# Sums of two gate quarters made in DRAM, and layer 2's first weights prepared at milestones, in a fused attention and two-layer kernel

## The chip, the cores and the metric

The kernel runs on one core of a Trainium2 chip. Its time is the device time of one execution in microseconds (us). Beside it stands one profiled execution, whose trace gives the start and the duration of the instructions of each engine: PE (TensorE, the matrix products), DVE (VectorE), ACT (ScalarE), POOL (GpSimd), and SP, which here only issues transfers. Each engine works through its own instructions in program order.

## The reference, cut to what matters

```python
attn = softmax(q @ k.T / 8 + cum[:, None] - cum[None, :], causal) @ v    # 4 x 8 heads, 576 positions, 64 wide
x  = attn.transpose(0, 2, 1, 3).reshape(2304, 512)
g  = leaky_relu(x @ w_in, 0.01)          # 512 -> 2048
x1 = g @ w_out                           # 2048 -> 512
h2 = x1 @ w2_in                          # 512 -> 2048
out = (h2 * sigmoid(h2)) @ w2_out        # 2048 -> 512
```

All of it is float32. The second product is `g @ w_out`; layer 2's first weights are `w2_in`.

## The kernel before, in words

A product in float32 is made of three passes in a split form: an operand is copied to a rounded high part (a cast on ACT) and the remainder is taken on DVE (`less`, line 373); high x high, high x low and low x high are added up in PSUM. The products after the first use Strassen's scheme in Winograd's form: seven products of quarters instead of eight, with sums and differences of quarters made on DVE.

The order of the instructions is written by a planner in the program itself: generators ask for an engine and a cost, wait for named signals, and a small event loop decides who issues next on each engine. So a wait that is added or dropped in one generator can move instructions of others, and the order is fixed when the program is built. Transfers issued by one engine also stand in that engine's order: one that must wait holds up the ones behind it.

The stages on PE, with lines: attention (L743, L824, L892) mixed with the first product (`hpw`, L960), to about 390 us; the second product `g @ w_out` (`acc`, L1218), from 392 us to 607 us, at first mixed with the last of the first product and at its end with the third; the third product (`m`, L1525), to 782 us; the fourth (`m`, L1667), to the end.

**The second product.** `g` is stored to DRAM (`g1_d`) by L1055 as 8 slabs (`NST`) for each of the 8 pieces of rows in `CHUNKS` (64 stores). It is read back in quarters, for three groups of 768 rows (`n` = 0, 1, 2). The quarters are named by rows and columns, 11, 12, 21 and 22; each comes in four pieces `s` (128 x 768 elements, 384 KB; the loads are L1091, tile `gq`). There is room for three quarters of a group. Quarter 21 of group n stands where 22 of group n-1 stood, and 22 where 12 stood. A piece's room is free again when its last reader is done: for 22 that is the preparation of product 4, for 12 that of product 3.

The seven products of a group are called by numbers `q` and come in the order 1, 5, 6, 2, 7, 4, 3 (1, 6, 5, 2, 7, 4, 3 from the second group on); product 1 of a group comes before products 4 and 3 of the group before it. For each, `prep` makes four split pieces in the tile `gs` (cast L1151, subtraction L373, four buffers `SPLITS`). `made` prepares two of the operands, in place: x5 = a21 + a22 (on DVE, L1117 by way of the helper line L1357) and x6 = x5 - a11 (L1120). Product 5 uses x5, product 6 uses x6, and products 2, 7 and 3 use operands built on x6. PE takes 12 matmuls of 384 columns for a piece, 6 for each half `j` of the columns. `("m1", n, j, q)` is the signal that product q of group n is made for half j.

**The weights of layer 2.** `fetch2` loads w2_in as packed words in eight pairs (two loads of 512 KB for a pair `j`, tile `wst`, L1881); `combos` decodes them (ACT L1712, DVE L1713, L1714, L1716), makes four sums and differences on DVE, and stores the pair to DRAM (`w_d<-f`, L1938, 896 KB) from one of two buffers. `fills` brings them back (`w<-w_d`, L1914) when a place is free; it also brings the 28 pieces of the second product's own weights.

**POOL** does 56 subtractions `m<-qk,m` (L369) for the heads of attention, and, after the first microseconds, nothing else.

Of the kernel before, what the change touches and what calls it, by code (L numbers as in the profile page):

```python
# [13 lines left out]
ALU = mybir.AluOpType  # L14
# [43 lines left out]
)  # L58
SPLITS = 4
INPUT_AT = 5  # L60
X_ON = "d"
SET_B = ("h", "h", ("acc", 0), ("acc", 1))


# [8 lines left out]
TB = 384  # L73
# [14 lines left out]
class Plan:  # L88
# [90 lines left out]
    def wait(self, *names):  # L179
        def step(resume):  # L180
            missing = [n for n in names if n not in self.seen]
            if not missing:
                resume()
                return
            left = [len(missing)]

            def one():
                left[0] -= 1
                if not left[0]:
                    resume()  # L190

            for n in missing:
                self.waiting.setdefault(n, []).append(one)

        return step
# [8 lines left out]
    def signal(self, name):  # L204
        self.seen[name] = True
        for fn in self.waiting.pop(name, []):
            fn()
# [79 lines left out]
def fused_kernel(ctx, tc, qt, kt, va, vb, ft, w1, wi2, wo2, out):  # L287
    nc = tc.nc
# [8 lines left out]
    SF = FF // 4  # L297
# [3 lines left out]
    NG = NT // (2 * TB)  # L301
# [389 lines left out]
    def loads():  # L691
        def line(todo):
            while todo:
                yield from load_head(todo.pop(0))

        todo = list(range(H, NSB * H))
        yield wait("cf")
        yield par(line(todo), line(todo))
# [368 lines left out]
    def quarter(grp, s):  # L1067
        return w2t["q", Q_AT[grp] + s // 2][:, s % 2]

    def q_group(n, name):  # L1070
        return {"11": 0, "21": 1 + n % 2, "12": 1 + n % 2, "22": 2 - n % 2}[name]

    def quarters():

        yield wait("decoded")
        todo = [(0, "11"), (0, "21"), (0, "22")]
        for n in range(NG):
            todo += [(n, "12")]
            if n + 1 < NG:
                todo += [(n + 1, "11"), (n + 1, "21"), (n + 1, "22")]  # L1080
        for n, name in todo:
            i, j = int(name[0]) - 1, int(name[1]) - 1
            o = (2 * n + i) * TB
            grp = q_group(n, name)
            for s in range(SF):
                sg = j * SF + s
                yield wait(*[("g1", k, sg) for k, (o1, n1) in enumerate(CHUNKS) if o1 < o + TB and o1 + n1 > o])
                yield take(("q", grp, s), 1)

                def load(n, name, s, sg, o, t):  # L1090
                    yield dma(393e3, lambda: nc.sync.dma_start(out=t, in_=g1_d[sg, :, :, o:o + TB]), 0)  # L1091
                    signal(("q", n, name, s))

                p.start(load(n, name, s, sg, o, quarter(grp, s)))

    g_order = sorted((7 * n + pos, n, q) for n in range(NG) for q, pos in G_TURN[n])
    gx = {}
# [14 lines left out]

    def made(n, s):

        a11, a21, a22 = (quarter(q_group(n, k), s) for k in ("11", "21", "22"))
        yield wait(("q", n, "21", s), ("q", n, "22", s))
        yield sub(2 * TB, a21, a21, a22, X_ON, 0, ALU.add)  # L1117
        signal(("x5", n, s))
        yield wait(("gx", n, 1, s))
        yield sub(2 * TB, a11, a21, a11, "d", 0)  # L1120
        signal(("x6", n, s))
        q_used(n, "21", s, 2)

    def prep(n, q, s, i):
        a = {k: quarter(q_group(n, k), s) for k in ("11", "12", "21", "22")}
        t = w2t["s", i % SPLITS]
        src, name = None, None
        if q == 1:
            yield wait(("q", n, "11", s))
            src = a["11"]  # L1130
        elif q == 5:
            yield wait(("x5", n, s))
            src = a["21"]
        elif q == 6:
            yield wait(("x6", n, s))
            src = a["11"]
        elif q == 7:
            yield wait(("x6", n, s))
            yield wait(("x3", n, s))
            yield sub(2 * TB, a["11"], a["22"], a["11"], "d", 0)  # L1140
            src = a["11"]
        elif q == 4:
            yield wait(("q", n, "22", s))
            src = a["22"]
        elif q == 2:
            yield wait(("q", n, "12", s))
            src = a["12"]
        else:
            yield wait(("x3", n, s))
            src = a["12"]  # L1150
        yield act(2 * TB, lambda: nc.scalar.copy(t[:, 0], src), 0, 0.09)  # L1151
        yield less(2 * TB, t[:, 1], src, f32(t[:, 0]), "d", 0, PE_LAT)
        gx[n, q, s] = t, i
        signal(("gx", n, q, s))
        if q == 5:
            q_used(n, "21", s, 2)
        elif q == 7:
            q_used(n, "22", s, 2)
            q_used(n, "11", s, 1)
        elif q == 4:  # L1160
            q_used(n, "22", s, 2)
        elif q == 2:
            yield wait(("x6", n, s))
            yield sub(2 * TB, a["12"], a["12"], a["11"], "d", 0)
            yield wait(("gx", n, 6, s))
            signal(("x3", n, s))
        elif q == 3:
            q_used(n, "12", s, 1)
# [185 lines left out]
    def sub(n, dst, a, b, engines="pd", rank=1, op_=ALU.subtract):  # L1354
        return p.either([c for c in (
            ("pool", pool_cost(n), lambda: nc.gpsimd.tensor_tensor(dst, a, b, op=op_), FAVOR),
            ("dve", dve_cost(n), lambda: nc.vector.tensor_tensor(dst, a, b, op=op_), 0.0),  # L1357
        ) if c[0][0] in engines], rank)
# [515 lines left out]
    def fetch2():  # L1874
        for which in range(2):
            if which:
                yield wait(("xc", 0, 3))
            for j in range(NP):
                for e in range(2):
                    st, i_st = yield from own([128, DM, 2], I32, "wst")  # L1880
                    yield dma(524e3, lambda: nc.sync.dma_start(  # L1881
                        out=st.rearrange("p n w -> p (n w)"), in_=(wi2, wo2)[which][j + NP * e].bitcast(I32)))
                    words2[which, j, e] = st, i_st
                    signal(("words2", which, j, e))
# [73 lines left out]
    def opening():  # L1958
        first_row["i"] = yield take("stg", STG_BUFS)
        first_row["tile"] = stg(first_row["i"], [H, 2, HALF[0][1]], F32, "cfr")  # L1960
        for i in range(5):
            yield take(("w", i), 1)
        p.start(gates(cp), after_gates)
        yield from load_first()
        yield wait(*[("weighed", n) for n in range(H)])
        for i in range(5):
            give(("w", i), 0)
# [3 lines left out]
        decp["wo"] = wo_es.enter_context(tc.tile_pool(name="wop", bufs=1))  # L1971

    with tc.manual_schedule():
        for gen in (opening(), first_weights(), loads(), attention(), hidden(), quarters(), preps(), summed(), all_fills(),
                    second_input(), second_weights(), hidden2(), second_values(), summed2()):
            p.start(gen)
        p.run()
# [51 lines left out]
```

## Time and profile before

| | |
|---|---|
| time, median of 3 runs | 960.33 us (959.15 to 962.2) |
| the profiled execution's own time | 963.02 us |
| its span, first to last instruction | 961.3 us |
| granted clock of TensorE, mean | 0.994 of full speed |
| busy: PE, DVE, ACT, POOL | 98%, 78%, 64%, 6% of the span |

The profiled execution took 2.7 us longer than the median, and 1.7 us of its time lie outside its span. Busy shares of PE count matmuls that overlap and whose ends are modelled, so the number of matmuls that start in a stretch says more than the share.

### The profile page before, as it was taken

How to read it: one execution, taken by the hardware profiler on the slowest of the kernel's cores; microseconds unless marked ns; L12 is line 12 of the kernel's file. 1: busy time of each engine (PE TensorE's matmuls, PEld its weight loads, DVE VectorE, ACT ScalarE, POOL GpSimd, SP SyncE). 2: the span in 40 equal slices, each digit the busy share in tenths (PEclk: the TensorE clock that was granted, in tenths of full speed). 3: DMA queues.
4: the chain of work that ended last, by engine and by line, in shares of the span. 5: the costliest groups of instructions: out<-in, count | busy, mean ns of one | idle time of the engine just before them, and what ended most of it. 6: DMA issues, size and time to landing. Idle time of an engine off the chain costs nothing.

```text
span 961.3 us, 18261 instructions
## 1 busy us (share of the span) xinstructions
PE 940.9 (98%) x6483; PEld 891.6 (93%) x6483; DVE 753.1 (78%) x1782; ACT 610.8 (64%) x1382; POOL 56.5 (6%) x71
## 2 busy tenths in 40 slices
PE   9999999999999999999989999999999999999998
PEld 7777998999888889999989899999999999999998
DVE  6998786689688962979999779858544498888885
ACT  7978787788588854666546359547556674444442
POOL 2001221122022100000000000000000000000000
PEclk9999999999999999999999999999999999999999
DMA  7943553466777656994956685797766683544542
GB/s 202 290 136 89 165 168 95 131 227 215 243 223 241 194 166 224 370 359 161 344 206 185 221 256 177 266 325 236 287 218 208 221 261 112 152 132 139 147 127 72
DMA packets 160023, 196.80 MB, mean 205 GB/s; under 512 B 9638, under 2 KB 145982, under 8 KB 159900
## 3 DMA queue, kind: packets, MB, share of 16 engines
q1 hardware_dynamic: 159500, 195.24, 63.5%
q8 instruction: 51, 0.84, 0.3%
q10 hardware_dynamic: 432, 0.39, 0.1%
q14 instruction: 40, 0.33, 0.1%
HBM read 125.94 MB, written 69.65 MB: 203 GB/s over the span
## 4 chain that ended last, share of the span: by engine, by line
PE 68%; DVE 13%; DMA 9%; ACT 5%; issue 3%; SPq 2%; POOL 0%; DVEq 0%; ACTq 0%; POOLq 0%
PE m L1667 18%; PE m L1525 18%; PE acc L1218 10%; PE hpw L960 10%; PE sps L743 4%; PE av L892 4%; PE tps L824 3%; DMA gq<-g_d 3%; DVE gq L1357 2%; DMA wst<-in_wi_dram 2%; ACT sc L766 1%; DVE sc L723 1%; DVE gs L373 1%; ACT sc L776 1%; PE hps L960 1%
## 5 line engine op out<-in xcount | busy, mean ns | idle before, releaser
L960 PE MATMUL hpw<-ring,w 128*128 128x320 f32 (+1 forms) x1344 | 218.0, 303 | 0.1
L960 PEld LDWEIGHTS hpw<-ring,w 128*128 128x128 f32 x1344 | 191.0, 190 | 2.4 <-issue 1.4
L1218 PE MATMUL acc<-gs,w 128*128 128x384 f32 x1008 | 186.2, 344 | 7.1 <-DVE gs L373 5.4
L1218 PEld LDWEIGHTS acc<-gs,w 128*128 128x128 f32 x1008 | 180.5, 191 | 10.2 <-DVE gs L373 6.5
L1525 PE MATMUL m<-xc,w 128*128 128x384 f32 x1008 | 180.3, 339 | 0.6 <-ACT m L1551 0.6
L1525 PEld LDWEIGHTS m<-xc,w 128*128 128x128 f32 x1008 | 177.6, 188 | 1.4 <-ACT m L1551 1.0
L1667 PE MATMUL m<-w,gc 128*128 128x256 f32 x1512 | 178.6, 280 | 0.0
L1667 PEld LDWEIGHTS m<-w,gc 128*128 128x128 f32 x1512 | 178.4, 188 | 0.0
L358 ACT CAST gc<-g 128x512 fp32r<-128x512 f32 (+1 forms) x180 | 80.0, 490 | 86.7 <-DVE g L1357 52.2
L1151 ACT CAST gs<-gq 128x768 fp32r<-128x768 f32 x84 | 69.8, 836 | 61.0 <-PE acc L1218 31.2
L766 ACT ACTIVATE sc<-sc,st 128x576 f32<-128x576 f32 (+4 forms) x160 | 92.9, 581 | 24.6 <-DVE st L723 23.6
L723 DVE CUSTOM_DVE_ANT_0 sc<-sps,zmask 128x288 f32<-128x288 f32 (+4 forms) x160 | 71.0, 448 | 31.1 <-PE sps L743 23.8
L373 DVE TENSOR_TENSOR gs<-gq,gs 128x768 fp32r<-128x768 f32 x84 | 79.4, 952 | 17.5 <-ACT gs L1151 16.9
L373 DVE TENSOR_TENSOR gc<-g,gc 128x512 fp32r<-128x512 f32 (+1 forms) x180 | 89.8, 525 | 3.3 <-ACT gc L358 1.9
L824 PE MATMUL tps<-ident,sc 66*107 66x66 f32 (+3 forms) x480 | 68.0, 269 | 3.8 <-ACT sc L776 1.8
L1357 DVE TENSOR_TENSOR g<-g 128x256 f32<-128x256 f32 x144 | 58.3, 418 | 16.7 <-DMA g<-g_d 16.2
L743 PE MATMUL sps<-m,s 66*128 66x288 f32 (+9 forms) x288 | 67.4, 315 | 3.2 <-DMA g_d<-gw 1.7
L369 POOL TENSOR_TENSOR m<-qk,m 64x288 fp32r<-64x288 f32 (+1 forms) x56 | 51.4, 930 | 275.2 <-ACT m L358 145.0
L373 DVE TENSOR_TENSOR w<-w 128x512 fp32r<-128x512 f32 x84 | 55.6, 686 | 14.6 <-ACT w L1915 14.4
L824 PEld LDWEIGHTS tps<-ident,sc 66*107 66x107 f32 (+3 forms) x480 | 55.2, 151 | 10.9 <-ACT sc L776 3.6
L1915 ACT CAST w<-w 128x512 fp32r<-128x512 f32 x84 | 50.7, 620 | 19.0 <-DMA w<-w_d 18.3
L1053 ACT ACTIVATE gw<-hpw 128x320 f32<-128x320 f32 (+1 forms) x112 | 44.7, 409 | 27.0 <-PE hpw L960 23.5
(124 smaller groups left out, 1113.3 us busy)
## 6 DMA issues: line engine op xcount, KB each, us to landing
w<-w_d SPq DMA_DIRECT2D x84, 256.0 KB
gq<-g_d SPq DMA_DIRECT2D x48, 384.0 KB
g_d<-z SPq DMA_DIRECT2D x24, 768.0 KB
g<-g_d SPq DMA_DIRECT2D x36, 512.0 KB
w_d<-f SPq DMA_DIRECT2D x16, 896.0 KB
g_d<-gw SPq DMA_DIRECT2D x32, 320.0 KB
wst<-in_w_dram SPq DMA_DIRECT2D x17, 512.0 KB
g_d<-gw SPq DMA_DIRECT2D x32, 256.0 KB
```

The costliest lines, as they stand in the source:

```text
L358: ("act", act_cost(n, base), lambda: nc.scalar.copy(dst, src), 0.0),
L373: ("dve", dve_cost(n), lambda: nc.vector.tensor_tensor(dst, a, b, op=ALU.subtract), 0.0),
L723: yield dve(w, lambda: nc.vector.tensor_tensor_reduce(out=sc[0:qn, k0:k0 + w], in0=ps[0:qn], in1=zmask[0:qn, z0:z0 + w], scale=-0.125, sca ...
L743: nc.tensor.matmul(ps[0:qn], ht[x][:, qs], ht[y][:, k0:k0 + w], start=r == 0, stop=r == len(ops) - 1)
L766: yield act(kn, lambda: nc.scalar.activation(sc[0:qn, 0:kn], sc[0:qn, 0:kn], ACTF.Exp, scale=-1.0, bias=st[0:qn, 2 * i + a:2 * i + a + 1], ...
L824: nc.tensor.transpose(ps[0:k1 - k0, o:o + qn], ht["p"][i][0:qn, k0:k1], ident[0:qn, 0:qn])
L960: nc.tensor.matmul(dst, w[:, wi, c * 128:(c + 1) * 128], x(xi, c), start=(first_ and c == 0 and r == 0), stop=(c == KC - 1 and r == 2), sk ...
L1151: yield act(2 * TB, lambda: nc.scalar.copy(t[:, 0], src), 0, 0.09)
L1218: nc.tensor.matmul(dst, w[:, e, wi, j * 128:(j + 1) * 128], x[:, xi, e], start=start and s == 0 and e == 0 and r == 0, stop=stop and s == ...
L1357: ("dve", dve_cost(n), lambda: nc.vector.tensor_tensor(dst, a, b, op=op_), 0.0),
L1525: nc.tensor.matmul(dst, w[:, wi, c * 128:(c + 1) * 128], x[:, xi, c], start=start and c == 0 and r == 0, stop=stop and c == 1 and r == 2, ...
L1667: nc.tensor.matmul(banks[b][:, e], t[:, gi, a * 128:(a + 1) * 128], w[:, wi], start=begin and a == 0 and r == 0, stop=jp == NP // 2 - 1 an ...
```

## The change

Two edits, and nothing of the arithmetic but the place where one sum is made.

First, x5 = a21 + a22 is no longer made by DVE. A new generator `added` issues twelve transfers on POOL's queue (three groups by four pieces), each of which adds the 384 KB of a piece of quarter 22 to the piece of quarter 21 within DRAM (`accum_op=ALU.add`), as soon as the stores of both are done. Quarter 21 is then loaded as the sum, after a wait for that transfer; quarter 22 is still loaded, for products 4 and 7. `made` makes only x6, and no longer waits for 22.

Second, `fetch2` waits before it loads pairs 2 to 7 of w2_in, for a milestone of the second product from the table `PACE`.

```diff
-X_ON = "d"
+PACE = {2: (0, 5), 3: (0, 2), 4: (0, 7), 5: (0, 3), 6: (1, 5), 7: (1, 7)}
...
+    def g1_made(n, i, sg):
+        o = (2 * n + i) * TB
+        return [("g1", k, sg) for k, (o1, n1) in enumerate(CHUNKS) if o1 < o + TB and o1 + n1 > o]
+
+    def added():
+        for n in range(NG):
+            o = (2 * n + 1) * TB
+            for s in range(SF):
+                yield wait(*g1_made(n, 1, s), *g1_made(n, 1, SF + s))
+                yield op("pool", 1.1, lambda: nc.gpsimd.dma_start(
+                    out=g1_d[s, :, :, o:o + TB], in_=g1_d[SF + s, :, :, o:o + TB], accum_op=ALU.add), 0, 10.0)
+                signal(("sum21", n, s))
+
     def quarters():
...
-                yield wait(*[("g1", k, sg) for k, (o1, n1) in enumerate(CHUNKS) if o1 < o + TB and o1 + n1 > o])
+                yield wait(*([("sum21", n, s)] if name == "21" else g1_made(n, i, sg)))
...
-        a11, a21, a22 = (quarter(q_group(n, k), s) for k in ("11", "21", "22"))
-        yield wait(("q", n, "21", s), ("q", n, "22", s))
-        yield sub(2 * TB, a21, a21, a22, X_ON, 0, ALU.add)
-        signal(("x5", n, s))
-        yield wait(("gx", n, 1, s))
+        a11, a21 = (quarter(q_group(n, k), s) for k in ("11", "21"))
+        yield wait(("q", n, "21", s), ("gx", n, 1, s))
         yield sub(2 * TB, a11, a21, a11, "d", 0)
...
         elif q == 5:
-            yield wait(("x5", n, s))
+            yield wait(("q", n, "21", s))
             src = a["21"]
...
             for j in range(NP):
+                if not which and j in PACE:
+                    yield wait(("m1", PACE[j][0], 0, PACE[j][1]))
                 for e in range(2):
...
-        for gen in (opening(), first_weights(), loads(), attention(), hidden(), quarters(), preps(), summed(), all_fills(),
+        for gen in (opening(), first_weights(), loads(), attention(), hidden(), added(), quarters(), preps(), summed(), all_fills(),
```

PE's instructions stand in the same order as before. The other engines' order changes; three places follow.

DVE, where the operands of product 6 of the last group are made. `gs_...` are the split pieces, `gq_...` the quarters; before, 5507 and 5508 hold quarter 21, 5505 and 5506 quarter 22, 5503 and 5504 quarter 11, and the `u` rows close products of the group before. Before:

```order
L373 TENSOR_TENSOR gs_5512<-gq_5506,gs_5512 128x768
L1357 TENSOR_TENSOR gq_5507<-gq_5507,gq_5505 128x768
L1357 TENSOR_TENSOR gq_5503<-gq_5507,gq_5503 128x768
L1357 TENSOR_TENSOR gq_5507<-gq_5507,gq_5505 128x768
L373 TENSOR_TENSOR gs_5509<-gq_5503,gs_5509 128x768
L1357 TENSOR_TENSOR gq_5508<-gq_5508,gq_5506 128x768
L1357 TENSOR_TENSOR gq_5503<-gq_5507,gq_5503 128x768
L1357 TENSOR_TENSOR gq_5508<-gq_5508,gq_5506 128x768
L1357 TENSOR_TENSOR gq_5504<-gq_5508,gq_5504 128x768
L1309 TENSOR_TENSOR u_6651<-acc_6700,u_6651 128x384
L1309 TENSOR_TENSOR u_6656<-acc_6701,u_6656 128x384
L373 TENSOR_TENSOR gs_5510<-gq_5503,gs_5510 128x768
```

In the changed program quarter 21 is in 5514 and 5515, quarter 11 in 5510 and 5511, and 5512 and 5513 hold quarter 12 of the group before, the operand of its product 3; `w2` are pieces of w2_in brought back:

```order
L1367 TENSOR_TENSOR gq_5510<-gq_5514,gq_5510 128x768
L373 TENSOR_TENSOR gs_5516<-gq_5512,gs_5516 128x768
L1367 TENSOR_TENSOR gq_5510<-gq_5514,gq_5510 128x768
L373 TENSOR_TENSOR gs_5517<-gq_5512,gs_5517 128x768
L1367 TENSOR_TENSOR gq_5511<-gq_5515,gq_5511 128x768
L373 TENSOR_TENSOR w2_6990<-w2_6990 128x2x256
L1367 TENSOR_TENSOR gq_5511<-gq_5515,gq_5511 128x768
L373 TENSOR_TENSOR gs_5518<-gq_5513,gs_5518 128x768
L373 TENSOR_TENSOR w2_7006<-w2_7006 128x2x256
L373 TENSOR_TENSOR gs_5519<-gq_5513,gs_5519 128x768
```

Four additions are gone, and the four subtractions of x6 moved from behind the last split of product 3 to before and between those splits.

DVE, the same place in the middle group. Before, 5508 is the last piece of quarter 12 of the group before (operand of its product 3), 5505 is quarter 21 of this group, 5507 quarter 22, 5503 quarter 11, and `f` are pairs of w2_in:

```order
L373 TENSOR_TENSOR gs_5512<-gq_5508,gs_5512 128x768
L1357 TENSOR_TENSOR f_6504<-f_6504 128x256
L1713 TENSOR_SCALAR f_6566<-f_6566 128x512
L1357 TENSOR_TENSOR f_6504<-f_6504 128x256
L1357 TENSOR_TENSOR gq_5505<-gq_5505,gq_5507 128x768 x2
L1357 TENSOR_TENSOR gq_5503<-gq_5505,gq_5503 128x768 x2
```

In the changed program 5512 and 5513 are first quarter 22 of the group before (operand of its product 4) and then, in the `gq` rows, quarter 21 of this group; 5514 is quarter 12 of the group before:

```order
L373 TENSOR_TENSOR gs_5516<-gq_5512,gs_5516 128x768
...
L373 TENSOR_TENSOR gs_5517<-gq_5512,gs_5517 128x768
L1367 TENSOR_TENSOR f_6238<-f_6238 128x256
L1726 SCALAR_TENSOR_TENSOR f_6337<-wst_6360,f_6337 128x512
L373 TENSOR_TENSOR gs_5518<-gq_5513,gs_5518 128x768
L1367 TENSOR_TENSOR gq_5510<-gq_5512,gq_5510 128x768
L1367 TENSOR_TENSOR f_6238<-f_6238 128x256
L1367 TENSOR_TENSOR f_6337<-f_6337 128x256
L373 TENSOR_TENSOR gs_5519<-gq_5513,gs_5519 128x768
L1367 TENSOR_TENSOR gq_5510<-gq_5512,gq_5510 128x768
L373 TENSOR_TENSOR gs_5516<-gq_5514,gs_5516 128x768
L1367 TENSOR_TENSOR gq_5511<-gq_5513,gq_5511 128x768
```

The first x6 now stands two splits after the split that frees the place of its quarter (the first row), among the splits of products 4 and 3.

POOL, where the first group's four transfers stand among the subtractions of heads (`m1_...`, one number a head), with what goes on both sides:

```order
-L369 TENSOR_TENSOR m1_2826<-qk_2825,m1_2826 64x256
-L369 TENSOR_TENSOR m1_3048<-qk_3047,m1_3048 64x288 x2
...
+L1082 DMA g1_d_77<-g1_d_77 256x384 x2
+L369 TENSOR_TENSOR m1_3049<-qk_3048,m1_3049 64x288 x2
+L369 TENSOR_TENSOR m1_3098<-qk_3097,m1_3098 64x288 x2
+L1082 DMA g1_d_77<-g1_d_77 256x384
+L369 TENSOR_TENSOR m1_3182<-qk_3181,m1_3182 64x288 x2
+L369 TENSOR_TENSOR m1_3291<-qk_3290,m1_3291 64x288 x2
+L1082 DMA g1_d_77<-g1_d_77 256x384
```

Head 2826's subtraction moved to DVE. The other eight transfers stand after POOL's last subtraction, so nothing is behind them.

## Rows read from the trace of the kernel before

**Rows 1.** The page's first part: busy time, share of the span, instructions.

```profile
PE 940.9 (98%) x6483; PEld 891.6 (93%) x6483; DVE 753.1 (78%) x1782; ACT 610.8 (64%) x1382; POOL 56.5 (6%) x71
```

**Rows 2.** Windows: length, busy us by engine (instructions), granted clock, DMA share, GB/s.

```profile
410.00:420.00 10.00, 10.00 (x69) 10.00 (x68) 4.48 (x9) 4.83 (x10) 0.00 (x0) 1.00 1.00 344
420.00:430.00 10.00, 10.00 (x59) 10.00 (x58) 9.44 (x16) 7.64 (x12) 0.00 (x0) 1.00 1.06 380
...
480.00:490.00 10.00, 6.88 (x32) 6.07 (x32) 10.00 (x14) 3.71 (x5) 0.00 (x0) 0.92 0.32 106
490.00:500.00 10.00, 10.00 (x54) 10.00 (x53) 8.38 (x15) 5.34 (x8) 0.00 (x0) 0.91 0.87 287
...
540.00:550.00 10.00, 7.86 (x44) 7.40 (x43) 9.71 (x12) 3.24 (x4) 0.00 (x0) 1.00 0.37 130
550.00:560.00 10.00, 10.00 (x50) 10.00 (x50) 5.65 (x7) 4.72 (x7) 0.00 (x0) 0.83 0.44 117
...
570.00:580.00 10.00, 10.00 (x59) 10.00 (x58) 10.00 (x13) 7.71 (x13) 0.00 (x0) 1.00 0.98 329
```

**Rows 3.** Timeline of PE: start, duration, what; in brackets idle before, what ended it.

```profile
394.10 0.97 PE L1218 MATMUL acc<-gs,w 128*128 128x384 f32 x4 [0.86 <-DVE w L373]
...
445.76 34.33 PE L1218 MATMUL acc<-gs,w 128*128 128x384 f32 x192 [0.97 <-DVE gs L373]
481.06 4.41 PE L1218 MATMUL acc<-gs,w 128*128 128x384 f32 x23 [0.97 <-DVE gs L373]
486.33 0.44 PE L1218 MATMUL acc<-gs,w 128*128 128x384 f32 x1 [0.85 <-ACT gs L1151]
488.07 4.27 PE L1218 MATMUL acc<-gs,w 128*128 128x384 f32 x14 [1.30 <-DVE gs L373]
549.36 3.13 PE L1218 MATMUL acc<-gs,w 128*128 128x384 f32 x10 [2.14 <-DVE gs L373]
```

**Rows 4.** The chain that ended last, 470 to 550 us: start, duration, what.

```profile
470.95 4.65 DMA gq<-g_d
476.06 3.47 DVE gq L1357 x4
...
531.82 8.29 DMA gq<-g_d
...
543.95 3.56 DVE gq L1357 x4
```

**Rows 5.** Groups by line: busy us, mean ns, idle before.

```profile
L1151 ACT CAST gs<-gq 128x768 fp32r<-128x768 f32 x84 | 69.8, 836 | 61.0 <-PE acc L1218 31.2 <-DVE gq L1357 22.9 <-DMA gq<-g_d 6.8
...
L1357 DVE TENSOR_TENSOR gq<-gq 128x768 f32<-128x768 f32 x48 | 44.1, 950 | 5.7 <-DMA gq<-g_d 5.6
```

**Rows 6.** The page's third part, the one queue that SP issues on.

```profile
q1 hardware_dynamic: 159500, 195.24, 63.5%
```

**Rows 7.** Timeline of SP: two stores of `g`, the first group's last and the last.

```profile
195.96 2.89 SPq L1055 DMA_DIRECT2D g_d<-gw  x2
...
421.47 0.52 SPq L1055 DMA_DIRECT2D g_d<-gw  x1
```

**Rows 8.** Timeline of POOL, three heads of attention.

```profile
203.92 1.84 POOL L369 TENSOR_TENSOR m<-qk,m 64x288 fp32r<-64x288 f32 x2 [12.48 <-ACT m L358]
208.78 2.16 POOL L369 TENSOR_TENSOR m<-qk,m 64x288 fp32r<-64x288 f32 x2 [3.01 <-PE tps L824]
213.70 2.01 POOL L369 TENSOR_TENSOR m<-qk,m 64x288 fp32r<-64x288 f32 x2 [2.76 <-ACT m L358]
```

**Rows 9.** Timeline of PE, where the first and the third of these heads begin.

```profile
209.38 0.46 PE L743 MATMUL sps<-m,s 128*66 128x320 f32 x2
...
222.55 0.46 PE L743 MATMUL sps<-m,s 128*66 128x320 f32 x2
```

**Rows 10.** Windows of DVE, line L359 (copies, casts), then L774 (products with a scalar).

```profile
190.00:230.00 40.00, 8.63 (x17) 1.00 0.74 238
...
190.00:230.00 40.00, 5.05 (x12) 1.00 0.74 238
```

## The prediction, made before the changed kernel ran

> **What bounds the kernel now.** The page's first part comes first: PE is busy for 940.9 of 961.3 us [rows 1], so the kernel is bound by PE, and a change can win only the 20 us in which PE waits and what PE loses while it runs slowly. The windows show where that is: at full pace a stretch of 10 us holds 58 or 59 matmuls of 384 columns, as from 570 us on, and I take 58.5 [rows 2]. Two places of the second product fall short of it. From 480 to 500 us 32 and 54 start, 86 in place of 117; from 540 to 560 us 44 and 50, 94 in place of 117. At 10/58.5 = 0.171 us each that is 5.3 us and 3.9 us lost.
>
> The timeline of PE says what ends the gaps: 0.97, 0.85 and 1.30 us at 481, 486 and 488 us, and 2.14 us at 549 us, each for a split piece of the second product, on DVE or ACT [rows 3]. After each place the granted clock is below 1: 0.92 and 0.91, then 0.83 [rows 2], which is time at the lower of the two levels, 1.2 in place of 2.4 GHz; it began once PE had stood still. Gap and clock add up: 3.12 + 0.8 + 0.9 = 4.8 us for the first place, 2.14 + 1.7 = 3.8 us for the second. The two ways of counting agree within 0.5 us; I carry 5.0 and 3.9.
>
> The chain of waits gives the cause. At the first place a load of a quarter takes 4.65 us, then DVE makes four additions or subtractions of quarters, 3.47 us; at the second a load takes 8.29 us and four such operations 3.56 us [rows 4], while DVE is busy for 10.00 and 9.71 of the 10 us [rows 2]. These are the operands of product 6: x5 needs quarters 21 and 22, and 22 can be loaded only when the last product of the group before has been prepared. So load, four additions and four subtractions stand in a row just ahead of PE.
>
> Two small gaps stand beside them: 0.86 us at 394 us, for a weight's split on DVE, and 0.97 us at 446 us [rows 3].
>
> **The change, part by part.** The additions: twelve operations of DVE at 0.950 us busy, which follow each other at some 0.87 us (3.47 us for four) [rows 4, 5], 10.4 us of DVE in all. Only those on the path count: 3.5 us at each of the two places and at the start. At the two places this alone is more than the gaps of 3.12 and 2.14 us.
>
> The wait for quarter 22 goes too. Product 6 then needs 21 alone, whose place is freed by product 4, one product earlier. One piece is 12 matmuls, 12 x 0.171 = 2.05 us, so a product is four pieces and the load can start some 8 us sooner. In the changed order x6 no longer stands in a block behind the last split of product 3, but between the splits. With both, I expect both stalls to go and the clock to stay up: -5.0 and -3.9 us. If only the gaps went and the clock still dipped, it would be 5.3 us in place of 8.9.
>
> The start: four additions (3.5 us) fewer ahead of the first weight splits, for which PE waited 0.86 us: -0.9 us. At 446 us eight operations on quarters remain, and pair 2 of w2_in, which stood among the splits ahead of them, comes later: between 0 and -1.0, I take -0.5.
>
> The milestones take no work away. Six pairs are decoded later and spread over the second product. The last milestone, product 7 of the middle group, stands nine products, 9 x 8.2 = 74 us, ahead of the second product's end, and the places into which the pieces are brought back come free only product by product in the last group. DVE has room for them: it is busy for 5.65 of 10 us from 550 us on [rows 2]. I cost this at nothing; if it were not hidden, a pair that comes late would hold the third product.
>
> What is added: twelve transfers that read two pieces of 384 KB and write one. Before has no transfer of POOL, so both their price and POOL's time to issue one are unknown. For the transfer: q1 moved 195.24 MB in 63.5% of 961.3 us, 320 GB/s while busy [rows 6], so one pass of 0.393 MB takes all engines 1.2 us; a transfer that adds is between one pass and three, 1.2 to 3.7 us. I take two, 2.5 us, as nearest to two reads beside one write. The first eight are due ahead of the second product. The last four wait for the last four stores, up to 421 us [rows 7], and fall into 410 to 430 us, where the transfer engines are at 1.00 and 1.06 of their time [rows 2]. Four times 2.5 us, less 1.6 us for a load of w2_in that has moved behind the weights, is 8 us more of transfers there (3 to 13). The second product's later weights come that much later, but PE needs the last of them, product 3's, only six products (49 us) after the first that runs alone, so only their place in DVE's order hurts: I take +1, with 0 and +6 as bounds.
>
> The Trainium skill, "Collectives: The Full Stack", on why ReduceScatter is half of AllGather, says that an adding transfer reads two sources on one ring and so costs twice a copy. By that the price would be the two passes that I took; no run here has shown it.
>
> POOL's issue: the nearest rows are its own subtractions, up to 2.16 us for two, and SP's issue of a store, 0.52 us [rows 7, 8]. I take 1 us, from 0.5 to 2.2. Behind the first two transfers stands a head's subtraction at 203.9 us, done at 205.8, which PE needs at 209.4; behind the third one at 213.7, done at 215.7, which PE needs at 222.6 [rows 8, 9]. The stores of all four are issued by 198.9 us, and those for the first two before 196.0 us [rows 7], so hardly a wait is left then. The gap ahead of the third is 2.76 us [rows 8]: 1 us fits, 2.2 us fit too. Cost nothing. That cover ends where an issue takes 2.76 + 6.8 = 9.6 us at the third, or, for two in a row from 196.0 us on, with a subtraction that may start as late as 203.9 + 3.6 = 207.5 us, (207.5 - 196.0) / 2 = 5.8 us.
>
> The new order adds a wait: x6 waits on DVE for its load, with the splits of products 4 and 3 behind it. In the middle group it stands two splits after the place is freed, 4.1 us; loads took 4.65 and 8.29 us [rows 4], so DVE is held for 0.5 to 4.2 us. Four buffers let a split be ready up to 3 x 2.05 - 0.84 - 0.95 = 4.4 us before PE uses it [rows 5], of which x6 itself takes 0.95. So PE loses between 0 and 0.8 us at a place; I take +0.5 for both.
>
> **The sum** is -5.0 - 3.9 - 0.9 - 0.5 + 1.0 + 0.5 = -8.8 us. The profiled execution would go from 963.0 to 954.2 us. It is 2.7 us above the median of the runs, and the stalls do not depend on that, so the median goes from 960.3 to **951.5 us**.
>
> **The rivals.** (A) The new wait is not covered. A load that takes 11 us, because pairs and weights are in flight with it, holds DVE for 7 us and PE for 3.5 us, with up to 1.5 us of slow clock behind it, at one or both places: 955 us, from 953 to 958. For it: 8.29 us was seen where the engines were loaded [rows 4]. Against it: the pairs are now spread, and the last group's first x6 stands behind more splits than the middle one's.
>
> (B) The last four transfers crowd out the weights. At three passes, 13 us more, the splits of weights in DVE's order hold back the pieces of products 6 and 2 of the first group: a stall of up to 6 us near 440 us, and 1.5 us of slow clock, in place of the 1 us that I took: 951.5 + 6.5 = 958 us, up to 962 if both sizes are short. For it: transfers at 1.06 [rows 2]. Against it: DVE was behind the fetches there, not ahead (9.44 of 10 us busy).
>
> (C) On the other side: POOL is held. If an issue takes 20 us rather than 1, two of them end at 236 us, the first head's subtraction is 32 us late against a cover of 3.6 us, and the third transfer adds up to 20 more: 951.5 + 28 to 48, some 985 us. It costs from 5.8 us an issue on, and the kernel is slower than before from 5.8 + 8.8 / 2 = 10.2 us on. For it: nothing in the trace bounds an issue by POOL itself. Against it: POOL's longest rows are 2 us.
>
> The Trainium skill has a rule that bears on it: "SBUF — State Buffer", who interferes with whom, says that GpSimd, which writes the descriptors of its transfers itself, is locked out while DVE copies, casts or multiplies by a scalar in its fast mode. In this kernel DVE spends 8.63 us of 190 to 230 us on copies and casts and 5.05 us on products with a scalar [rows 10], a third of the time together. An issue stretched by that third is 1.5 us in place of 1 and 3.3 in place of 2.2, still covered; by that rule the sum stays, and (C) gets no more than its chance.
>
> (D) The pacing fails: a pair is late and the third product waits near 600 us. Each us late is one us lost; 5 us late gives 956.5.
>
> **How the numbers follow.** Forecast 0.65, A 0.14, B 0.12, C 0.05, D 0.04. The forecast's own range is 949 (-11.1 if every gap goes, at no cost) to 954. For 8 in 10 the range goes over A and part of B: 948.5 to 958. A measurement of this kernel can tell some 0.3%, 2.9 us, from no change: faster is below 957.4 us, slower above 963.2. Faster holds the forecast, A and D nearly whole and a third of B: 0.85. Same takes the rest of B and the tails: 0.08. Slower is C and the worst of B: 0.07.
>
> **What would show it.** Right: 115 to 118 matmuls from each of the two places' 20 us, clock at 1.00, no gap over 0.5 us there; the second product ending 8 to 10 us earlier, the third and fourth as long as before; twelve fewer DVE additions; POOL's issues at 1 to 2 us. The prediction is wrong if a gap of over 1 us stands at x6 with a load before it (A), near 440 us behind a weight (B), at an `sps` behind POOL (C) or at the third product's start (D).

## The result, and the profile after

The changed kernel took 968.4 us (median of 6 runs, 966.6 to 971.5), the one before, on the same chip, 961.2 us (957.5 to 963.1). The ratio is 1.0079, 95% interval 1.0059 to 1.0099: slower, by 7.6 us, where 951.5 us and a gain of 8.8 us had been forecast. The profiled execution took 971.5 us, the longest of the six, so its trace loses some 3 us more than a typical run does.

The stretches first, of the kernel after (length, busy us and instructions by engine, granted clock, DMA share, GB/s):

```profile
230.00:240.00 10.00, 7.82 (x42) 7.07 (x43) 6.65 (x20) 5.95 (x16) 0.70 (x1) 0.83 0.45 157
340.00:350.00 10.00, 10.00 (x76) 8.78 (x76) 5.32 (x13) 3.74 (x9) 1.75 (x2) 1.00 0.93 220
350.00:360.00 10.00, 3.28 (x25) 3.03 (x24) 1.89 (x5) 1.65 (x5) 0.88 (x1) 0.74 0.78 215
440.00:450.00 10.00, 5.25 (x26) 4.23 (x24) 5.30 (x8) 4.87 (x8) 0.00 (x0) 0.85 1.10 301
450.00:460.00 10.00, 9.87 (x46) 9.87 (x47) 10.00 (x14) 6.29 (x11) 0.00 (x0) 0.81 0.34 139
480.00:500.00 20.00, 20.00 (x115) 20.00 (x114) 15.04 (x24) 9.11 (x13) 0.00 (x0) 1.00 0.86 286
540.00:560.00 20.00, 19.65 (x112) 19.33 (x111) 18.96 (x27) 12.09 (x19) 0.00 (x0) 1.00 0.85 270
```

The two stalls of [rows 2, 3] are away: 115 and 112 matmuls where there were 86 and 94. Three new holes stand in their place, and the timeline of PE of the kernel after shows them (start, duration, what, idle before, what ended it):

```profile
235.59 1.42 PE L824 MATMUL tps<-ident,sc 66*106 66x66 f32 x6 [1.90 <-DVE st L723]
...
358.74 0.90 PE L824 MATMUL tps<-ident,sc 128*128 128x128 f32 x3 [6.72 <-ACT pf L358]
...
442.91 2.20 PE L1228 MATMUL acc<-gs,w 128*128 128x384 f32 x11 [0.55 <-DVE gs L373]
449.14 0.69 PE L1228 MATMUL acc<-gs,w 128*128 128x384 f32 x1 [4.03 <-ACT gs L1161]
```

PE's order is the same in both kernels, so one can ask, for each matmul, how much later it starts after than before. Counted from the matmuls of the stretches 0 to 10 us, 0 to 20 us and so on:

| before's clock, us | 180 | 240 | 290 | 310 | 340 | 360 | 430 | 440 | 480 | 500 | 540 | 560 | 830 | 950 |
|---|---|---|---|---|---|---|---|---|---|---|---|---|---|---|
| after is later by, us | -1.3 | 4.3 | 4.5 | 1.4 | 1.9 | 8.3 | 8.2 | 14.8 | 14.6 | 9.1 | 9.6 | 6.3 | 6.6 | 7.7 |

The forecast's gains are there: -5.5 us from 480 to 500 us and -3.3 us from 540 to 560 us (forecast -5.0 and -3.9). But 5.6 us are lost from 180 to 240 us, 6.4 us from 340 to 360 us and 6.6 us from 430 to 440 us. (The -1.3 us at the start and a good part of the 3.1 us that before loses from 290 to 310 us belong to that one execution of before: the profiles of e1 and e15 below, which do the same work there, are 0.7 and 1.0 us ahead of it at 180 us and gain another 1.4 and 2.0 us from 290 to 310 us.)

Each loss lies where transfers of POOL run; those of the first group were issued from 187.7 to 221.7 us. The timeline of POOL after, its issues of the new transfers from the second group on, with what each waited for:

```profile
336.98 0.87 POOL L1082 DMA_DIRECT2D g_d<-g_d  x1
343.19 0.88 POOL L1082 DMA_DIRECT2D g_d<-g_d  x1 [5.34 <-DMA g_d<-gw]
348.45 0.87 POOL L1082 DMA_DIRECT2D g_d<-g_d  x1 [4.39 <-DMA g_d<-gw]
358.35 0.88 POOL L1082 DMA_DIRECT2D g_d<-g_d  x1 [9.02 <-DMA g_d<-gw]
422.09 0.88 POOL L1082 DMA_DIRECT2D g_d<-g_d  x1 [62.86 <-DMA g_d<-gw]
433.56 0.88 POOL L1082 DMA_DIRECT2D g_d<-g_d  x1 [10.59 <-DMA g_d<-gw]
435.74 0.88 POOL L1082 DMA_DIRECT2D g_d<-g_d  x1 [1.30 <-DMA g_d<-gw]
437.94 0.88 POOL L1082 DMA_DIRECT2D g_d<-g_d  x1 [1.32 <-DMA g_d<-gw]
```

An issue costs POOL 0.9 us (0.85 to 1.16), near the forecast of 1 (its subtractions: [rows 8]). What waits is another queue: the chain that ended last, after, has long transfers of SP just there, among them these three, and behind two of them the casts that they hold:

```profile
225.57 9.05 DMA qk<-in_kt_dram
...
345.39 11.83 DMA w_d<-wf
357.38 0.67 ACT wf L1722
...
428.94 7.63 DMA w<-w_d
436.60 0.62 ACT w L1927
```

The one at 345 us shows it best. The store of a finished pair of w_out takes 11.83 us; before, at the same step (343.27 us), it took 6.40 us:

```profile
343.27 6.40 DMA w_d<-wf
```

There is one buffer `wf`, so the next cast into it waits on ACT, which serves in order, and attention's `pf` stands behind it. ACT's waits after, from 335 to 362 us and from 415 to 460 us (us in total, times, longest):

```profile
ACT wf L1722 <- DMA w_d<-wf: 11.3, 1, 11.3
```

```profile
ACT w L1927 <- DMA w<-w_d: 10.6, 8, 3.5
```

Before, the same two waits were 5.8 and 3.0 us. The first, of before:

```profile
ACT wf L1712 <- DMA w_d<-wf: 5.8, 1, 5.8
```

And the price of one transfer, from the page's queues after (q1 as in [rows 6], and a new one):

```profile
q1 hardware_dynamic: 159500, 195.24, 63.0%
q0 software_dynamic: 3264, 4.72, 3.3%
```

Twelve transfers take 3.3% of the 969.6 us of all 16 transfer engines, 2.67 us each; the forecast had 2.5. The four of a group are 10.7 us of transfer time put in among the work of q1.

### The profile page after: what moved, and what is told of

Read it like the earlier page. It is cut to its first block, busy times and chain, and to the rows that moved or that the text cites. A ratio compares the mean times of both kernels' runs of the same rounds, so it can differ in the third digit from the quotient of the medians.

```text
span 969.6 us, 18269 instructions
## 1 busy us (share of the span) xinstructions
PE 943.7 (97%) x6483; PEld 893.2 (92%) x6483; DVE 744.9 (77%) x1771; ACT 611.6 (63%) x1382; POOL 65.2 (7%) x82
## 4 chain that ended last, share of the span: by engine, by line
PE 65%; DVE 14%; DMA 10%; ACT 6%; issue 4%; SPq 1%; DVEq 0%; ACTq 0%
PE m L1677 18%; PE m L1535 17%; PE hpw L960 10%; PE acc L1228 5%; PE sps L743 4%; PE av L892 4%; PE tps L824 3%; DVE gs L373 3%; DMA w<-w_d 2%; DVE gq L1367 2%; DMA w_d<-f 2%; DMA qk<-in_kt_dram 2%; ACT sc L766 2%; DVE sc L723 1%; DMA gq<-g_d 1%
## 5 line engine op out<-in xcount | busy, mean ns | idle before, releaser
L369 POOL TENSOR_TENSOR m<-qk,m 64x288 fp32r<-64x288 f32 (+1 forms) x55 | 49.4, 909 | 269.8 <-ACT m L358 133.0
```

## The experiments

Theory 1: the adding transfers delay SP's transfers, which share the engines, and PE loses where such a transfer is due soon. Rivals: the new order of DVE, ACT and SP does it and the transfers are bystanders (2); four such transfers cost the same wherever they stand (3). Ratios are to before on the same chip (median 959.0 to 959.6 us for e1 to e16).

| run | time, us | ratio, 95% interval |
|---|---|---|
| after | 968.4 | 1.0079 (1.0059 to 1.0099) |
| e1 no sums | 951.4 | 0.9922 (0.9898 to 0.9945) |
| e2 plain copies | 956.0 | 0.9960 (0.9942 to 0.9977) |
| e3 milestones alone | 955.0 | 0.9952 (0.9929 to 0.9975) |
| e4 first on DVE, others held late, tiles 32 bytes on | 970.3 | 1.0120 (1.0098 to 1.0142) |
| e5 second group early, others on DVE, tiles 32 bytes on | 944.3 | 0.9829 (0.9805 to 0.9853) |
| e6, e7, e8 first, second, third group alone | 953.0, 957.2, 957.5 | 0.9928 (0.9908 to 0.9949), 0.9968 (0.9951 to 0.9985), 0.9967 (0.9948 to 0.9986) |
| e9 before, tiles 32 bytes on | 950.5 | 0.9901 (0.9865 to 0.9936) |
| e10 as e5, tiles in place | 953.3 | 0.9930 (0.9905 to 0.9954) |
| e11 as e3, tiles 32 bytes on | 944.6 | 0.9840 (0.9809 to 0.9872) |
| e12 no sums, no milestones | 951.7 | 0.9919 (0.9892 to 0.9945) |
| e13 after, tiles 32 bytes on | 957.9 | 0.9980 (0.9962 to 0.9998) |
| e14 second early, third at 455 us | 957.7 | 0.9984 (0.9973 to 0.9994) |
| e15 before, tiles 64 bytes on | 959.5 | 1.0003 (0.9978 to 1.0029) |
| e16 before, data 32 bytes back, new order on DVE | 946.2 | 0.9867 (0.9846 to 0.9888) |

**e1: the transfers left out.**

```diff
-for gen in (..., hidden(), added(), quarters(), ...
+for gen in (..., hidden(), quarters(), ...
-    yield wait(*([("sum21", n, s)] if name == "21" else g1_made(n, i, sg)))
+    yield wait(*g1_made(n, i, sg))
```

> The twelve adding transfers are left out and nothing takes their place: quarter 21 is loaded as it is, so products 5, 6, 2, 7 and 3 get operands without the sum. DVE's orders, the milestones and the loads stay as in the changed kernel. Theory 1 (the transfers delay SP's transfers on the same engines, in three places): the changed kernel falls behind the one before by 5.5 us in 190 to 240 us, 6.4 us in 340 to 350 us and 6.5 us in 430 to 450 us, 18.4 us together, and all of it goes: 968.4 - 18.4 = 950 us, from 947 to 954, with the spill at 345 us back from 11.8 to about 6.4 us and no gap of over 1 us near 443 us. Theory 2 (the new order of DVE, ACT and SP makes weights and pairs late, the transfers are bystanders): the gaps at 359 and 449 us stay, 963 to 969 us.

951.4 us. The transfers cost 1.0079 - 0.9922 = 1.6%, 15 us. The store takes 6.29 us again, and PE runs from 429.76 us on for 30 us without a gap:

```profile
341.82 6.29 DMA w_d<-wf
429.76 30.54 PE L1228 MATMUL acc<-gs,w 128*128 128x384 f32 x172
```

In the two traces DVE, ACT and SP issue the same work in the same order, but for one subtraction of a head that goes back from DVE to POOL. Nor is it the new wait of the loads of quarter 21, which e1 drops too: after, those of the second and third group are issued from 475 and 536 us on, behind the holes at 359 and 449 us. Theory 2 falls.

**e2: the same bytes, not added.**

```diff
-    ..., in_=g1_d[SF + s, :, :, o:o + TB], accum_op=ALU.add), 0, 10.0)
+    ..., in_=g1_d[SF + s, :, :, o:o + TB]), 0, 10.0)
```

> The twelve transfers stay, with their waits and sizes, but copy quarter 22 over quarter 21 and add nothing, so the operands hold 22 in place of the sum. Theory 1 with adding as the price: an adding transfer takes 2.67 us of all engines (3.3% of 969.6 us over twelve), 147 GB/s against 320 GB/s of the other queue; a copy should take about 1.2 to 1.5 us and the three losses shrink to about a third to a half: 953 to 960 us. Theory 1 with the path (from DRAM to DRAM, or POOL's queue) as the price: 965 to 969 us, the queue's share stays near 3.3%.

956.0 us: copies cost 0.4% where adding costs 1.6%. The page's queues of e2:

```profile
q0 software_dynamic: 1344, 4.72, 1.5%
```

For the same bytes that is 1.19 us a transfer in place of 2.67, and 112 packets in place of 272; the store near 341 us takes 7.35 us. It is the adding that makes them long. The loss shrinks to a quarter, more than the transfers do; that would fit a wait that begins only beyond some slack, which no run measures.

**e3: the milestones alone, e12: the sums away without milestones.** e3 is before with the two lines of `PACE` in `fetch2`; e12 is e1 without them.

```diff
+                if not which and j in PACE:
+                    yield wait(("m1", PACE[j][0], 0, PACE[j][1]))
```

> The kernel before with the milestones alone; DVE adds x5 as before. Prediction's step: the milestones cost nothing, and the stalls at 480 and 540 us belong to load and additions ahead of product 6, so they stay: 960 us, from 957 to 963. Rival: the stalls came from the pairs, decoded by DVE at 460 to 500 and 525 us, and go with the milestones alone: 952 to 955 us, and the adding transfers were never needed.

> The kernel before with quarter 21 loaded as it is: no additions on DVE, no transfers, no milestones. The fourth corner of a square: before 959.6, milestones alone 955.0, milestones without sums 951.4 us. Prediction's step (additions and the load of quarter 22 made both stalls, milestones cost nothing and bring nothing): 951 us. If each half brings its own: 955 to 957 us. If the milestones must be there first: 958 to 960 us.

955.0 and 951.7 us. With e1 (951.4) that is a square: without the additions the milestones bring nothing, with them they bring 4.6 us (0.48%). In e3 the gaps near 480 and 486 us stay (1.24 and 1.56 us), the one at 549 us goes. DVE does not decode less beside the additions: its work on `f` from 440 to 560 us is 28.2 us before and 30.4 us in e3. What differs is its order. Before, four operations on quarters stand in a block at 543.95 us [rows 4], ahead of the split that PE waits for; in e3 they stand one at a time (the rows left out are short sums that close a product):

```profile
541.00 0.95 DVE L374 TENSOR_TENSOR gs<-gq,gs 128x768 fp32r<-128x768 f32 x1
541.87 0.95 DVE L1358 TENSOR_TENSOR gq<-gq 128x768 f32<-128x768 f32 x1
...
543.20 0.95 DVE L1358 TENSOR_TENSOR gq<-gq 128x768 f32<-128x768 f32 x1
...
544.53 0.95 DVE L374 TENSOR_TENSOR gs<-gq,gs 128x768 fp32r<-128x768 f32 x1
```

Near 474 us e3 still has a block of five (4.58 us), and there the gaps stay. That the order is the cause is read from the traces; no run changes it alone. Windows of e12:

```profile
480.00:500.00 20.00, 20.00 (x115) 20.00 (x114) 19.40 (x31) 9.50 (x13) 0.00 (x0) 1.00 0.78 260
540.00:560.00 20.00, 20.00 (x115) 20.00 (x114) 15.51 (x19) 10.02 (x15) 0.00 (x0) 1.00 0.77 239
```

So the additions, and the wait for quarter 22 with them, did make both stalls; e12 is 7.8 us (0.81%) ahead of before.

**e6 to e8: one group's transfers each**, with the other groups' sums left out (here e7's first line):

```diff
-        for n in range(NG):
+        for n in (1,):
```

> The changed kernel with the first group's adding transfers alone; quarter 21 of the other two groups is loaded without the sum. Without any it took 951.4 us. Theory 1: the loss of 190 to 240 us stays, 5.5 us, the others go: 957 us, from 954 to 959. If the losses are no property of the place but of the whole (a queue that is slow once POOL issues): nearer to 951 or to 968 than to 957.

> The same with the middle group's adding transfers alone, issued at some 337 to 358 us. Theory 1: the spill at 343 us lands late and the cast behind it holds ACT, 5.4 to 6.4 us: 957 us, from 954 to 960. If the first group's shift of all later work was what brought the spill and the transfers together: 952 us.

> The same with the last group's adding transfers alone, issued at some 413 to 430 us among the second product's weights. Theory 1: a gap of 4 us for a split near 440 us with slow clock behind it, 6.5 us: 958 us, from 954 to 960. Prediction's step as it stood: +1 us, 952 us.

Against e1 the first group costs 0.06% (not to be told from nothing), the second 0.46%, the third 0.45%: 0.6, 4.4 and 4.3 us, together 9 of the 15. PE's gaps, of e7 and then of e8:

```profile
354.25 0.90 PE L824 MATMUL tps<-ident,sc 128*128 128x128 f32 x3 [6.51 <-ACT pf L358]
```

```profile
437.25 0.60 PE L1228 MATMUL acc<-gs,w 128*128 128x384 f32 x1 [3.20 <-ACT gs L1161]
```

Both are the holes of the kernel after, at their places, each with its own group alone. The store near 341 us, of e7 and then of e8:

```profile
341.06 11.68 DMA w_d<-wf
```

```profile
340.65 6.09 DMA w_d<-wf
```

The 5.6 us that the profile of after lost from 180 to 240 us are no steady price: those of e6 and e13 lose 2.4 and 2.7 us there. The other 6 of the 15 us were not taken apart. Part of them may lie in e1 itself: from 860 to 930 us its profile starts 592 matmuls, as after's does, those of e6 to e8 598 or 599, which is worth 1.2 us by the end. If the other runs do the same, each of the three prices is 1.2 us higher and some 2 us are left, an estimate.

**e4, e5, e10, e14: other times.** DVE adds x5 of some groups as before (`ON_DVE`); POOL is held back by a small subtraction that reads a tile which is ready late. e4 (group 0 on DVE) reads a split piece of product 4 of the first group ahead of group 1, and one of product 5 of the second ahead of group 2. e5 (groups 0 and 2 on DVE) and e10 read the last pair of w_out ahead of group 1; e14 does so too, and ahead of group 2 reads product 4 of the first group.

```diff
+            if n in EARLY_SUMS:
+                yield wait("mixed")
+                f = last["wf"]
+                yield op("pool", 0.2, lambda: nc.gpsimd.tensor_tensor(
+                    mark, f[:, 6, 0:8], f[:, 6, 8:16], op=ALU.subtract), 0)
```

> DVE adds x5 of the first group as before; the sums of the other two stay transfers, held back by a subtraction of eight columns on POOL that reads a split piece of product 4 of the first group (about 437 us) and of product 5 of the second (about 460 us). Theory 1: the losses at 190 to 240 us, 340 to 350 us and 430 to 450 us go, and what the transfers cost at their new places is small as long as SP's engines have room there (0.31 and 0.72 of their time at 440 to 460 us before): 951 us, from 948 to 957. Theory 3 (an adding transfer costs PE about as much wherever it stands): 968.4 - 5.5 = 963 us.

> Milestones as in the changed kernel; DVE adds x5 of the first and third group as before, and only the middle group's sums are adding transfers, held back on POOL until the last pair of w_out is mixed, some 357 us, so that they run at 357 to 370 us, where the transfer engines were at 0.18 and 0.36 of their time before. Theory 1 (an adding transfer costs what it delays on the other queue, nothing where there is room): the remaining gaps of the milestones alone, 1.24 and 1.56 us at 480 and 486 us with their slow clock, go as well: 952 us, from 950 to 955, below the 955.0 us of the milestones alone. Theory 3 (four adding transfers cost 5 to 6 us anywhere): 957 to 961 us.

> The kernel that took 944.3 us, with the eight columns of the held-back subtraction in room that is free there anyway, so that no tile lies 32 bytes further. If the place gave the rate: 598 matmuls from 860 to 930 us and 944.3 + 7.5 = 952 us, from 949 to 955; the stalls at 480 and 540 us as in the run before. If the early sums gave it: 944 us.

> No tile is shifted. DVE adds x5 of the first group, the middle group's sums run from 354 us on as in e10, and the last group's are held back on POOL until product 4 of the first group is being split, some 450 us. Theory 1 (an adding transfer costs what it delays): free at its new place, the gap of 3 to 4 us near 440 us is away: 952 us, from 949 to 955, beside 953.3 us with the middle group alone. If the last group's four transfers cost their 6 us wherever they stand: 958 to 960 us.

e4 was a miss, 970.3 us: the marks came at 453 and 480 us, the sums' loads behind them, and PE stood still for what was late. Its timeline of PE:

```profile
491.28 0.69 PE L1241 MATMUL acc<-gs,w 128*128 128x384 f32 x1 [12.55 <-ACT gs L1174]
```

e10 is the test of the place for the second group. POOL's timeline of e10:

```profile
355.21 0.20 POOL L1086 TENSOR_TENSOR mark<-wf 128x8 f32<-128x8 f32 x1 [21.97 <-DVE wf L1379]
355.72 4.41 POOL L1090 DMA_DIRECT2D g_d<-g_d  x4 [0.32 <-issue]
```

The same four transfers that e7 issues from 333 to 354 us, at a cost of 4.4 us, come from 356 us on, all of them past the store, which takes 5.99 us, and the kernel takes 953.3 us; a new gap of 1.73 us at 376 us, for a split of the first quarters, is likely what they still cost. Theory 3 falls for this group. But the run is not safely better than the milestones alone (0.9930 against 0.9952, intervals that overlap): the relief of DVE may be worth no more than what the transfers still take. e14 missed its range: from 455 us on, the third group's transfers run beside loads of quarters, one of 10.88 us, and PE waits 2.49 us at 471 us for a split. It is 0.5% above e10; no other place was tried for the third group, so none was found that is free.

**e9, e11, e13, e15, e16: where the tiles lie.** e4 and e5 had a new tile of 32 bytes ahead of the others, and both ran the last product faster, so e9 did that alone (e15 with 64 bytes, e11 on e3, e13 on the changed kernel). e16 puts 32 bytes at the other end, so that data move and weights stay; the small operation on DVE that fills them (0.07 us) has also changed the order of DVE, ACT and SP between 404 and 550 us, so only the third and fourth product of e16 show the place alone.

```diff
+    const.tile([128, 8], F32, name="room")
```

> The kernel before, and nothing else than 32 bytes a partition that are reserved ahead of the other tiles and never used, as the two kernels with the subtraction of eight columns had them. Both of those started 619 matmuls from 860 to 930 us, in a stretch without a gap, where before starts 598 and the changed kernel 592. Theory of the place: all tiles lie 32 bytes further and PE runs the fourth product 3.5% and the third 1.5% faster, 619 from 860 to 930 us and 952 us in all, from 950 to 954. Theory of the order (the rate came with something that those two kernels do): 959.5 us and 598 matmuls.

> The milestones alone, all sums on DVE, and the unused 32 bytes. If the place gives 7.5 us to any order: 955.0 - 7.5 = 947.5 us, from 945 to 950, and what the early sums of the middle group are worth is the distance to 944.3 us: 3 us (the gaps of 1.24 and 1.56 us with their slow clock). If place and order do not add up: 951 to 955 us.

> The changed kernel and the unused 32 bytes of e9. If the rate that comes with the place adds to everything else: 968.4 - 8.6 = 960 us, from 957 to 962, and the three losses (190 to 240, 340 to 350, 430 to 450 us) stand as they were. If the changed kernel's 592 matmuls from 860 to 930 us had another cause that the shift does not lift: 967 us.

> The kernel before with 64 unused bytes in place of 32. If what counts is where the weights lie within 64 bytes, the rate is that of before: 598 matmuls from 860 to 930 us, 959 us. If any shift away from the old place helps: 619 and 951 us.

> The kernel before with 32 bytes (filled once by DVE) at the far end of the room, so that the data operands of the last three products lie 32 bytes lower and the weights where they were; both then begin at a multiple of 64. If what counts is that weights and data lie alike within 64 bytes (in e9 both stood 32 past a multiple of 64, in before weights 0 and data 32): 619 matmuls from 860 to 930 us and 951 us. If the weights' own place counts: 598 and 959 us.

The fourth product from 860 to 930 us, of before, e9, e15 and e16:

```profile
860.00:930.00 70.00, 70.00 (x598) 70.00 (x598) 60.55 (x142) 31.70 (x73) 0.00 (x0) 1.00 0.48 136
```

```profile
860.00:930.00 70.00, 70.00 (x618) 70.00 (x618) 62.39 (x147) 33.66 (x78) 0.00 (x0) 1.00 0.47 136
```

```profile
860.00:930.00 70.00, 70.00 (x594) 70.00 (x593) 58.89 (x140) 32.22 (x74) 0.00 (x0) 1.00 0.46 135
```

```profile
860.00:930.00 70.00, 70.00 (x619) 70.00 (x618) 61.85 (x145) 32.95 (x77) 0.00 (x0) 1.00 0.46 134
```

PE is never idle in any of them and the clock is at 1.00, yet some 3.5% more matmuls start where weights and data begin alike within 64 bytes (e9: both 32 past a multiple; e16: both at one) than where they don't (before and e15: data 32 past). All six kernels with a move of 32 bytes start 618 or 619 there, the twelve others 592 to 599; in the third product, from 640 to 760 us, it is 688 to 692 against 674 to 681. It adds to the rest: e9 against before, e13 against after and e5 against e10 are each 1.0%, e11 against e3 1.1%, with the same order on every engine. The 1.3% of e16 are not the place alone: its new order also breaks up the block of four ahead of PE's gap at 549 us, as e3's does, with no milestone and no transfer.

**Best.** e11 (944.6 us) and e5 (944.3 us) beat both kernels and cannot be told apart: the milestones and 32 unused bytes, with the sums on DVE, are enough.

## Why the prediction was wrong

**The stalls.** Right: load, additions and subtractions ahead of product 6 made them, and without the additions they go, at a clock of 1.00. By the starts of its matmuls e12 gains 5.4 us from 480 to 500 us and 4.0 us from 540 to 560 us on before, where 5.0 and 3.9 were forecast. The whole is 7.8 us and not the 10.3 of the four terms; 1.2 us of the difference is e12's last product, which starts 592 matmuls from 860 to 930 us where before's starts 598.

**The milestones.** Nothing beside the transfers' form of the sum, as forecast (e1, e12). That they would bring 4.6 us with the additions on DVE, most of what the change wanted, was not seen.

**A transfer's own price, and POOL's issue.** 2.67 us were forecast as 2.5, and 0.9 us as 1. The Trainium skill, "Collectives: The Full Stack", on why ReduceScatter is half of AllGather, puts the adding transfer of a collective at twice a copy, for its two source reads. Here it is 2.67 against 1.19 us (e2), 2.2 times. Rival (C) did not come.

**What failed** is the step "The first eight are due ahead of the second product", which put eight transfers at nothing, and the one behind it, "so only their place in DVE's order hurts: I take +1". Due ahead of the second product is not the same as in a free stretch: the forecast asked when the sums were needed, and not what q1 had in flight when they ran. At 343 us that was the store of the single buffer `wf`, for which ACT already waited 5.8 us; the trace of before had it. For the last four, rival (B) had the mechanism (late weights, slow clock) and its price of 6 us, but was set aside because "DVE was behind the fetches there"; ACT, ahead of DVE in a weight's split, waited 3.0 us for fetches even before, and 10.6 us after. Nor did it take the three passes that (B) asked for: four transfers of 2.67 us made the stall. One term of +1 was 15 us (1.6%, e1), of which e7 and e8 place 4.4 and 4.3 us. These 14 us, and 2 us of gain that did not come (7.5 in e1 in place of 9.8), are the whole distance from -8.8 to +7.6 us.

The Trainium skill, "DMA: Bandwidth & Descriptors", on queues, rings and completion order, says that a transfer engine takes turns between the queues that have work for it, a packet at a time. The store at 345 us, 11.83 us beside POOL's transfers and 6.29 us without them (e1), agrees. By that rule work on a second queue slows whatever the first one has in flight.

**The wait of x6 on its load** (+0.5) shows no gap above 0.5 us from 480 to 500 or 540 to 560 us in the kernel after; rival (A) did not come, nor (D).

**Open.** The 2 to 6 us of the 15 that the groups one by one do not show; whether any place is free for the third group's transfers; and why kernels with the same places of tiles start 592 to 599 matmuls from 860 to 930 us (after and e1 592, before 598), which is 1.1 us of the 7.6 (the table's last two columns).

## What to carry to other kernels

Work that is moved from a busy engine to the transfer engines is priced by what it delays there: list every transfer that is in flight while it runs, and find the one that somebody waits for, above all a store that frees a single buffer. A sum made twelve times off the critical engine was worth 8 us and cost 15; a mere delay of the decoding, free of transfers, took more than half of the gain at no price, by a new order on DVE as far as the traces show. And before a change of order is judged by a per cent, make sure that no tile has moved.

## What the runs showed of the hardware

The place of the operands decides the rate of TensorE in the float32 products of 256 columns: 598 against 618 matmuls in 70 us at the same clock, and with the third product some 1.0% of the whole time for a move of 32 bytes of all tiles (e9, e13, e5 against e10). A move of the data alone, the other way, gives the same rate (619, e16). It was fast where weights and data began alike within 64 bytes, and slow where not; that is three places of the two operands and no more, and no cause is shown. Nor does the rule hold matmul by matmul: in before, one of the 28 pieces of weights lies at 32 like the data, and its 54 matmuls, in runs of three, start 118 ns apart like the rest.

A transfer of 384 KB within DRAM took 2.67 us of all transfer engines when it added and 1.19 us when it copied (after, e2), and a store of 896 KB beside such transfers 11.5 to 11.8 us when they added, 7.35 us when they copied and 5.9 to 6.4 us without them.
